# The cast of twelve weights' high part on GpSimd instead of ScalarE, in an attention and mixer kernel

## The chip, the cores and the metric

The kernel runs on one core of one Trainium2 chip. The metric is the device time of one execution in microseconds. A core has five engines with an instruction queue each: TensorE (PE; its weight load is listed apart as PEld), VectorE (DVE), ScalarE (ACT), GpSimd (POOL) and SyncE (SP), which here issues the DMAs. GpSimd works on SBUF only, not on PSUM, in this kernel.

## The reference

Attention within chunks of 64 positions for 8 batches, 8 heads, 576 positions and head size 64, and then a mixer over the result:

```python
x    = attention(q, k, v)                      # per chunk of 64, [8, 576, 512], float32
xt   = x.transpose(0, 2, 1)
h    = np.maximum(xt @ w_tok1, 0.0) @ w_tok2   # over the 576 tokens, hidden size 256
u    = x + h.transpose(0, 2, 1)
h2   = np.maximum(u @ w_ch1, 0.0) @ w_ch2      # over the 512 channels, hidden size 1536
out  = u + h2
```

The four weights come as 64-bit floats. "First channel product" means `u @ w_ch1`, "second channel product" the one with `w_ch2`.

## The kernel before, in words

TensorE multiplies numbers of a reduced format, fp32r. To keep the precision of float32, each float32 operand is split into a high part (the operand cast to fp32r) and a low part (the operand minus the high part, again in fp32r). A product is then three matmuls into one PSUM tile: high by high, low by high, high by low (the list `THREE`).

The channel weights are cut into twelve slices each along the hidden size of 1536: `c1` slices for the first product and `c2` slices for the second, each 128 partitions by 512. They arrive as pairs of 32-bit words of a 64-bit float (`raw`), and are turned into float32 and split once, at the start of the program, in the order c1 0, c1 1, c2 0, c1 2, c2 1, ... Each slice passes these steps (line, engine, tile):

1. `words_scalar`: the upper words scaled into `wtop` (L189) and the lower words into `low` (L190), both on ScalarE
2. `words_clamp`: `wtop` clamped on VectorE (L196) and cast into the other half of `low` on ScalarE (L199)
3. `words_shift`: `wtop` shifted on VectorE (L203)
4. `words_add`: `low` added to `wtop` on VectorE (L209, a custom instruction); `wtop` then holds the float32 weight
5. `split_high`: the high part, `wtop` cast into `kept[:, 0]` on ScalarE (L251 for c1, L254 for c2 and for the token weights)
6. `split_low`: the low part, `wtop - kept[:, 0]` into `kept[:, 1]` on VectorE (L262)

`wtop` has four buffers, and one is free again after step 6. The generator `conversion` staggers the steps of successive slices: the clamp of slice i, shift and add and high part of slice i-1, low part of slice i-2. The token weights (`t1`, `t2`) pass steps 1 to 4 at the very start, and are split later, through the same functions.

Beside this, TensorE works on the first batch's 576 rows in two halves of 288: for each of the twelve slices, `ch1` computes the first product of both halves (L663, PSUM `ps_c`) and `ch2` the second of the first half (L705, PSUM `acc`). Between them, the result of the first product is rectified and split: its high part `gh` on ScalarE (L674), its low part `gl` on VectorE (L675); the second half's result is kept as `g` (L671) and split later (L685, L686). Attention of the second batch is spread over the same time: scores (L313), maximum, difference and exponential (L329, L332, L336), the transposed probabilities `pt` (L407), the product with v (L426), the division (L447), a transposition through memory (L379 and DMAs), and the split of the result, `xh` on ScalarE (L467) and `xl` on GpSimd (L468). After that come seven further stretches of rows, the later ones with sums of slices (`ring`), in which no weight of the input is converted any more; GpSimd helps there with additions and low parts (L653, L716, L988, L997, L1004, L1077, L1111, L1121).

What sets the order: the queues of TensorE, ScalarE and VectorE are written out by hand up to the first token products (about 45 us). Then a planner that simulates the program orders these queues, until TensorE's is written by hand again for the later rows. SyncE's queue is in program order throughout; GpSimd's is the planner's throughout.

Of the kernel before, what the change touches and what calls it, by code (L numbers as in the profile page):

```python
# [91 lines left out]
def attention_mixer_kernel(ctx, tc, qk_in, vo_in, v_in, w1_in, w2_in, wc1_in, wc2_in, out):  # L92
# [19 lines left out]
    nc = tc.nc  # L112
# [33 lines left out]
    weights, tops, lows = {}, {}, {}  # L146
# [78 lines left out]
    def conversion():  # L225

        for i in range(len(plan) + 2):
            if i < len(plan):
                prepare(i + 1 - len(prepared))
                words_clamp(i)  # L230
                yield
            if 0 < i <= len(plan):
                words_shift(i - 1)
                yield
            if 0 < i <= len(plan):
                words_add(i - 1)
                if i - 1 >= token:
                    split_high(i - 1)
                yield
            if token <= i - 2:  # L240
                split_low(i - 2)
                yield

    def split_high(i):

        key, _, _, n = plan[i]
        name = "kept_" + "_".join(map(str, key))
        kept = ctx.enter_context(tc.tile_pool(name=name, bufs=1, reuse_waits="tile"))
        if key[0] == "c1":
            parts = kept.tile([P, 2, 2, KH], F32R, name=name).rearrange("p j w n -> p w j n")  # L250
            nc.scalar.copy(out=parts[:, 0], in_=tops[i].rearrange("p (j n) -> p j n", j=2))  # L251
        else:
            parts = kept.tile([P, 2, n], F32R, name=name)
            nc.scalar.copy(out=parts[:, 0], in_=tops[i])  # L254
        tops[key, "parts"] = parts

    def split_low(i):
# [570 lines left out]
    def split(i):  # L828
        with ExitStack() as late:
            for engine in (nc.scalar.engine, nc.vector.engine):  # L830
                late.enter_context(tc.issue_after(last_of[engine]))
            split_high(i)
            split_low(i)
            if plan[i][0][0] == "t1" and ("t1", 4) in weights and not half_low:
                kept_half = const.tile([P, 2, DT], F32R, name="half_low")
                half_all.append(kept_half)
                for c in range(2):
                    nc.vector.tensor_scalar(
                        out=kept_half[:, c], in0=weights["t1", 4][:, 1].bitcast(F32),
                        scalar1=half_mask[:, c:c + 1], scalar2=None, op0=ALU.mult,  # L840
                    )
                    half_low.append(kept_half[:, c])
# [483 lines left out]
```

## Time and profile before

| | |
|---|---|
| median of 3 runs | 772.92 us (770.47, 772.92, 773.38) |
| the profiled execution | 771.12 us, span 769.3 us |
| busy: TensorE | 751.5 us |
| busy: VectorE, ScalarE, GpSimd | 440.4, 275.8, 193.8 us |
| the twelve `c2` casts | 34.4 to 99.2 us from the span's start |
| granted TensorE clock | 0.999 of full speed |

A row of a timeline gives start and duration in us, the engine, the line of the kernel, the operation, the tile written and those read, the shapes, the number of instructions, and in brackets the idle time of the engine before it with what ended it. A row of groups gives busy time in all, the mean of one in ns, and the idle time before them. A row of one line gives the shortest, median and longest duration in ns.

### The profile page before, as it was taken

The numbers are of one execution on the slowest core, as the hardware profiler recorded it, in microseconds if no ns is written. First come the engines' busy times: TensorE is split into PE (matmuls) and PEld (weight loads), VectorE is DVE, ScalarE is ACT, GpSimd is POOL, SyncE is SP. The second block draws the span as 40 slices with busy tenths as digits, with TensorE's granted clock in tenths as the row PEclk, the third lists the DMA queues.
The fourth block names the chain that finished last, engine by engine and source line by source line (L and its number), as shares of the span: only waits on it lengthen the run. The fifth ranks groups of instructions, "written<-read, shape, count | busy, mean of one in ns | idle before, by whom it ended". The sixth has DMA issues, their size and how long they took to land.

```text
span 769.3 us, 14611 instructions
## 1 busy us (share of the span) xinstructions
PE 751.5 (98%) x5742; PEld 631.9 (82%) x5742; DVE 440.4 (57%) x735; ACT 275.8 (36%) x505; POOL 193.8 (25%) x163
## 2 busy tenths in 40 slices
PE   7899999999999999999999999999999999999997
PEld 4589998878888887888888888988888888888886
DVE  5898946646537456596567653875344458333351
ACT  6899933332223334243242222432112133111310
POOL 0000002343446544021111162141212504212121
PEclk9999999999999999999999999999999999999999
DMA  9956245677945776828878872056344512534011
GB/s 356 407 211 216 76 152 194 214 244 245 294 151 183 219 238 194 260 73 262 277 250 271 270 251 72 2 188 209 126 156 145 172 49 86 188 124 148 4 52 51
DMA packets 93268, 139.94 MB, mean 182 GB/s; under 512 B 10832, under 2 KB 44880, under 8 KB 93200
## 3 DMA queue, kind: packets, MB, share of 16 engines
q1 hardware_dynamic: 93200, 139.02, 54.9%
q8 instruction: 45, 0.74, 0.4%
q14 instruction: 23, 0.19, 0.1%
HBM read 98.34 MB, written 39.71 MB: 179 GB/s over the span
## 4 chain that ended last, share of the span: by engine, by line
PE 84%; DVE 5%; ACT 5%; DMA 2%; issue 2%; SPq 1%; POOL 0%; POOLq 0%; ACTq 0%; DVEq 0%
PE acc L1098 25%; PE ps_p L1031 22%; PE acc L705 10%; PE ps_c L663 8%; PE ps_t L635 7%; PE ps_t L565 6%; PE ps_sv L356 2%; PE ps_sv L368 2%; DVE wtop L209 1%; PE sum L574 1%; ACT low L199 1%; ACT wtop L189 1%; ACT low L190 1%; DMA raw_t<-in_w 1%; DVE blocks L379 1%
## 5 line engine op out<-in xcount | busy, mean ns | idle before, releaser
L1098 PE MATMUL acc<-gh,kept_c 128*128 128x512 f32 (+1 forms) x576 | 176.2, 387 | 0.0
L1031 PE MATMUL ps_p<-bh,ring 128*128 128x512 f32 (+1 forms) x504 | 154.3, 387 | 0.0
L1098 PEld LDWEIGHTS acc<-gh,kept_c 128*128 128x128 f32 x576 | 107.4, 188 | 20.6
L1098 PE MATMUL acc<-gl,kept_c 128*128 128x512 f32 (+1 forms) x288 | 111.1, 386 | 0.0
L1031 PEld LDWEIGHTS ps_p<-bh,ring 128*128 128x128 f32 x504 | 94.0, 188 | 18.2
L1031 PE MATMUL ps_p<-bl,ring 128*128 128x512 f32 (+1 forms) x252 | 97.2, 386 | 0.0
L705 PE MATMUL acc<-gh,kept_c 128*128 128x288 f32 (+1 forms) x384 | 95.3, 347 | 1.0 <-ACT gh L674 1.0
L468 POOL TENSOR_TENSOR xl<-x,xh 128x512 fp32r<-128x512 f32 x28 | 38.6, 1392 | 165.7 <-ACT xh L467 154.5
L705 PEld LDWEIGHTS acc<-gh,kept_c 128*128 128x128 f32 x384 | 64.0, 188 | 9.9 <-ACT gh L674 1.4
L1121 POOL TENSOR_TENSOR sum<-snap,sum 128x512 f32<-128x512 f32 (+1 forms) x18 | 23.5, 1305 | 180.2 <-ACT snap L1116 165.6
L1098 PEld LDWEIGHTS acc<-gl,kept_c 128*128 128x128 f32 x288 | 54.0, 188 | 10.4
L705 PE MATMUL acc<-gl,kept_c 128*128 128x288 f32 (+1 forms) x192 | 60.4, 343 | 1.2 <-DVE gl L686 1.2
L663 PE MATMUL ps_c<-uh,kept_c 128*128 128x512 f32 x192 | 59.8, 393 | 0.0
L1031 PEld LDWEIGHTS ps_p<-bl,ring 128*128 128x128 f32 x252 | 47.3, 188 | 9.0
L336 ACT ACTIVATE pr<-pr 128x512 f32<-128x512 f32 x36 | 22.8, 632 | 81.3 <-DVE pr L332 77.3
L1126 ACT ACTIVATE gh<-c 128x512 fp32r<-128x512 f32 (+1 forms) x36 | 22.4, 623 | 81.8 <-DVE c L1121 78.2
L1116 ACT COPY snap<-ps_p 128x512 f32<-128x512 f32 (+1 forms) x36 | 20.8, 578 | 82.2 <-PE ps_p L1031 82.2
L675 DVE SCALAR_TENSOR_TENSOR gl<-ps_c,gh 128x512 fp32r<-128x512 f32 (+1 forms) x36 | 21.7, 604 | 46.2 <-ACT gh L674 46.1
L1127 DVE SCALAR_TENSOR_TENSOR gl<-g,gh 128x512 fp32r<-128x512 f32 (+1 forms) x36 | 33.2, 951 | 22.2 <-ACT gh L1126 16.4
L663 PE MATMUL ps_c<-both,kept_c 128*128 128x288 f32 x288 | 43.9, 298 | 0.1
L663 PEld LDWEIGHTS ps_c<-uh,kept_c 128*128 128x128 f32 x192 | 35.5, 188 | 7.5 <-DVE rl L583 0.2
L663 PEld LDWEIGHTS ps_c<-both,kept_c 128*128 128x128 f32 x288 | 39.6, 188 | 0.8 <-ACT g L671 0.3
(134 smaller groups left out, 1272.4 us busy)
## 6 DMA issues: line engine op xcount, KB each, us to landing
ring<-w SPq DMA_DIRECT2D x126, 256.0 KB, 4.1
qk<-in_qk SPq DMA_DIRECT2D x36, 512.0 KB, 5.3
far<-blocks SPq DMA_DIRECT2D x63, 256.0 KB, 3.0
raw_c<-in_wc SPq DMA_DIRECT2D x24, 512.0 KB, 9.6
pf<-far SPq DMA_DIRECT2D x124, 64.0 KB, 2.7
v<-in_v SPq DMA_DIRECT2D x27, 256.0 KB, 5.3
xt<-far SPq DMA_DIRECT2D x96, 64.0 KB, 2.1
w<-sparts SPq DMA_DIRECT2D x24, 256.0 KB, 2.8
```

The source lines that it names most:

```text
L336: nc.scalar.activation(out=pr, in_=pr, func=AF.Exp, scale=1.0 / float(D) ** 0.5)
L468: nc.gpsimd.tensor_tensor(out=xl, in0=t["own"], in1=xh.bitcast(F32), op=ALU.subtract)
L565: nc.tensor.matmul(ps, lhsT=lhsT, rhs=rhs, start=(n == 0 and q == 0), stop=(n == len(mt) - 1 and q == len(terms) - 1),)
L635: nc.tensor.matmul(ps[:, at:at + n], lhsT=lhsT[:, cols], rhs=rhs, start=(q == 0), stop=(q == len(terms) - 1),)
L663: nc.tensor.matmul(ps[:, :width], lhsT=weights["c1", f][:, wi, k // 2, k % 2 * P:(k % 2 + 1) * P], rhs=u[ui][k], start=(k == 0 and q == 0) ...
L675: nc.vector.scalar_tensor_tensor(out=gl, in0=ps[:, :width], scalar=0.0, in1=gh.bitcast(F32), op0=ALU.max, op1=ALU.subtract)
L705: nc.tensor.matmul(accs[e], lhsT=weights["c2", f][:, wi, e * P:(e + 1) * P], rhs=g[gi], start=(f == 0 and q == 0), stop=(f == NFC - 1 and ...
L1031: nc.tensor.matmul(ps, lhsT=w[:, wi, j * P:(j + 1) * P].bitcast(F32R), rhs=u[ui][j], start=j == 0 and q == 0, stop=j == 1 and q == 2,)
L1098: nc.tensor.matmul(accs[e], lhsT=weights["c2", f][:, wi, e * P:(e + 1) * P], rhs=g[gi], start=start and q == 0, stop=stop and q == 2,)
L1121: (engine or nc.vector).tensor_tensor(out=c, in0=a, in1=b, op=ALU.add)
L1126: nc.scalar.activation(out=gh, in_=c, func=AF.Relu)
L1127: nc.vector.scalar_tensor_tensor(out=gl, in0=c, scalar=0.0, in1=gh.bitcast(F32), op0=ALU.max, op1=ALU.subtract)
```

## The change

In `split_high`, the high part of the `c2` slices is written by GpSimd's `tensor_copy` instead of ScalarE's `copy`. The `c1` slices and the token weights keep ScalarE.

```diff
         else:
             parts = kept.tile([P, 2, n], F32R, name=name)
-            nc.scalar.copy(out=parts[:, 0], in_=tops[i])
+            if key[0] == "c2":
+                nc.gpsimd.tensor_copy(out=parts[:, 0], in_=tops[i])
+            else:
+                nc.scalar.copy(out=parts[:, 0], in_=tops[i])
         tops[key, "parts"] = parts
```

## The prediction

> **What bounds the kernel now.** I read the busy shares first, then the chain, then a table of stretches around the changed casts, then what the matmul queue waited for.
>
> ```profile
> span 769.3 us, 14611 instructions
> PE 751.5 (98%) x5742; PEld 631.9 (82%) x5742; DVE 440.4 (57%) x735; ACT 275.8 (36%) x505; POOL 193.8 (25%) x163
> PE 84%; DVE 5%; ACT 5%; DMA 2%; issue 2%; SPq 1%; POOL 0%; POOLq 0%; ACTq 0%; DVEq 0%
> ```
>
> TensorE is busy for 751.5 of 769.3 us, so all its gaps together are 17.8 us, and no help to another engine can give more. The 10% of the chain that runs over VectorE and ScalarE lies in the first part. The next answer cuts the span into stretches: length, then busy time (and instructions) of PE, weight load, DVE, ACT, POOL, then granted clock, DMA share and GB/s.
>
> ```profile
> 34.00:100.00 66.00, 64.52 (x570) 58.52 (x569) 59.59 (x122) 62.24 (x118) 2.99 (x2) 1.00 0.52 182
> 100.00:125.00 25.00, 23.50 (x222) 22.11 (x222) 13.15 (x28) 9.32 (x23) 5.11 (x5) 1.00 0.51 152
> 125.00:245.00 120.00, 119.17 (x1074) 100.08 (x1073) 64.78 (x108) 37.07 (x72) 46.24 (x40) 1.00 0.67 224
> 350.00:769.30 419.30, 413.85 (x2549) 348.01 (x2547) 214.72 (x321) 104.62 (x188) 99.82 (x74) 1.00 0.47 152
> ```
>
> The change works in 34 to 100 us. There ScalarE (62.24 of 66) and VectorE (59.59 of 66) are both nearly full, GpSimd is empty (2.99), and yet TensorE is busy for 64.52. Its waits, longest first (total us, times, longest), in 34 to 125 us:
>
> ```profile
> PE acc L705 <- DVE gl L686: 1.2, 1, 1.2
> PE acc L705 <- ACT gh L674: 1.0, 3, 0.4
> PE ps_v L426 <- ACT pt L407: 0.6, 2, 0.4
> ```
>
> So 2.8 us of TensorE's time in this stretch were spent waiting for the engines that the change touches, 1.6 us of it directly for ScalarE. That is the ceiling of the gain there.
>
> **The change part by part.**
>
> *Removed from ScalarE: twelve casts.*
>
> ```profile
> L254 ACT CAST kept_c<-wtop x12: 617/625/705, 34.4 to 99.2; 128x512 fp32r<-128x512 f32 x12
> 80.33 0.66 ACT L254 CAST kept_c<-wtop 128x512 fp32r<-128x512 f32 x1
> 80.84 0.84 ACT L190 ACTIVATE low<-raw_c 128x512 int16<-128x512 uint32 x1
> ACT kept_c L254 <- DVE wtop L209: 2.1, 4, 0.7
> ```
>
> One lasts 0.625 us, but the next instruction starts 0.51 us after it (80.33 to 80.84), so ScalarE gets 12 x 0.51 = 6.1 us back, and also the 2.1 us in which it stood at these casts for VectorE's add. Its 62.24 us become some 56 of 66. On TensorE's path this is worth at most the 1.6 us of waits for gh and pt; those waits also hang on VectorE (ScalarE's order holds casts and exponentials that wait for it), so I take a third, -0.5 us, between 0 and -1.6. The line's five other casts (the token weights) stay on ScalarE. No DMA is issued by the step, and none reads the twelve tiles: SyncE's queue is not touched.
>
> *Added on GpSimd: twelve casts of 128x512.* The trace has no GpSimd instruction with one input. The nearest rows on that engine have two inputs of the same size:
>
> ```profile
> L988 POOL TENSOR_TENSOR wsum<-kept_c x12: 1277/1294/1746, 154.7 to 283.4; 128x512 f32<-128x512 f32 x12
> 110.05 1.29 POOL L468 TENSOR_TENSOR xl<-x,xh 128x512 fp32r<-128x512 f32 x1 [14.82 <-ACT xh L467]
> 124.85 0.40 PE L565 MATMUL ps_t<-xl,kept_t 128*128 128x512 f32 x1
> ```
>
> I bound the cast by ScalarE's 0.62 us below and by 1.29 us above, and take 0.9 us, near the middle: the engine is the slower one, but has half as much to read. That is 12 x 0.9 = 10.8 us (7.4 to 15.5) on an engine with 63 us free in the stretch. Queued behind the casts stand GpSimd's subtractions for the token product; the third starts at 110.05, and TensorE first reads one at 124.85, so a delay of a cast or two is covered by 13 us.
>
> [...]
>
> *Added: a new wait.* The subtraction of line 262 on VectorE now waits for GpSimd. Behind it in VectorE's order stand the next weights' steps and the low halves gl that TensorE reads. What it has to spare is seen in these rows:
>
> ```profile
> 81.79 0.67 DVE L262 TENSOR_TENSOR kept_c<-wtop,kept_c 128x512 fp32r<-128x512 f32 x1
> 98.44 0.68 DVE L209 CUSTOM_DVE_ANT_0 wtop<-wtop,low 128x1024 uint16<-128x1024 uint16 x1
> 99.04 0.45 DVE L675 SCALAR_TENSOR_TENSOR gl<-ps_c,gh 128x288 fp32r<-128x288 f32 x1
> 100.03 0.64 DVE L262 TENSOR_TENSOR kept_c<-wtop,kept_c 128x512 fp32r<-128x512 f32 x1
> 100.87 0.56 PE L705 MATMUL acc<-gl,kept_c 128*128 128x288 f32 x3
> 108.88 1.74 PE L663 MATMUL ps_c<-both,kept_c 128*128 128x288 f32 x12
> ```
>
> The cast at 80.33 has its subtraction at 81.79, 1.46 us after its start; the last weight's add ends at 99.12 and its subtraction starts at 100.03, 0.91 us later. A cast of 0.9 us fits in both; one of 1.29 us would hold the last by some 0.4 us. The weights themselves are ready early: the last is complete at 100.67, while the last group but one of the first channel product starts at 108.88 and the second product's use comes after it. A conversion that ends 8 us late is therefore hidden. Cover that is thin is gl's: it is done at 99.49 and read at 100.87, 1.4 us.
>
> *Added: GpSimd in VectorE's way.* In the stretch GpSimd ran twice, and both times a VectorE instruction was long:
>
> ```profile
> 72.36 1.69 POOL L468 TENSOR_TENSOR xl<-x,xh 128x512 fp32r<-128x512 f32 x1 [70.83 <-ACT xh L467]
> 73.11 1.21 DVE L196 TENSOR_SCALAR wtop<-wtop 128x512 f32<-128x512 f32 x1 [0.23 <-ACT wtop L189]
> 93.93 1.30 POOL L468 TENSOR_TENSOR xl<-x,xh 128x512 fp32r<-128x512 f32 x1 [19.89 <-ACT xh L467]
> 94.06 1.72 DVE L209 CUSTOM_DVE_ANT_0 wtop<-wtop,low 128x1024 uint16<-128x1024 uint16 x1
> 95.87 0.62 ACT L254 CAST kept_c<-wtop 128x512 fp32r<-128x512 f32 x1 [0.52 <-DVE wtop L209]
> L196 DVE TENSOR_SCALAR wtop<-wtop x24: 373/418/1214, 24.7 to 93.4; 128x512 f32<-128x512 f32 x24
> L209 DVE CUSTOM_DVE_ANT_0 wtop<-wtop,low x24: 643/682/1718, 28.9 to 98.4; 128x1024 uint16<-128x1024 uint16 x24
> ```
>
> Against their medians the two lost 1.214 - 0.418 = 0.80 and 1.718 - 0.682 = 1.04 us, each until shortly after GpSimd's instruction ended (74.05 and 95.23); ScalarE then stood 0.52 us at 95.87. Together 1.83 us for two GpSimd instructions of 1.29 us undisturbed: 0.71 us lost per us held. Twelve casts of 0.9 us would cost VectorE 12 x 0.9 x 0.71 = 7.7 us (5.3 at 0.62 us, 11.0 at 1.29 us; if each held VectorE for all its length, 15.5; nothing, if it always found VectorE in another kind of work, but these four groups are most of the stretch):
>
> ```profile
> L209 DVE CUSTOM_DVE_ANT_0 wtop<-wtop,low 128x1024 uint16<-128x1024 uint16 x22 | 15.9, 726 | 0.2
> L262 DVE TENSOR_TENSOR kept_c<-wtop,kept_c 128x512 fp32r<-128x512 f32 x22 | 14.9, 678 | 0.2
> L196 DVE TENSOR_SCALAR wtop<-wtop 128x512 f32<-128x512 f32 x20 | 9.0, 455 | 4.0 <-ACT wtop L189 3.8
> L203 DVE TENSOR_SCALAR wtop<-wtop 128x512 int32<-128x512 int32 x21 | 8.6, 417 | 1.0 <-ACT low L199 1.0
> ```
>
> 15.9 + 14.9 + 9.0 + 8.6 = 48.4 of 59.59 us. VectorE has 66 - 59.59 = 6.4 us free, 4.8 of it waiting for ScalarE's own steps, which the change brings earlier. So 7.7 us overrun it by 1.3 us, about what gl's 1.4 us of cover takes. I charge +0.9 us on TensorE's path for places where cover is thinner (0 to 7.7 us, below).
>
> [...]
>
> *Sum.* -0.5 + 0.9 = +0.4 us. The profiled execution took 771.12 us (span 769.3 and 1.8 us around it); the runs shown are 770.47, 772.92 and 773.38, so it lies 1.8 us under their median. With the four executions' mean of 771.97 the sum gives 772.4 us, no measurable change.
>
> **The rivals.**
>
> *VectorE becomes the bound (slower).* Place: 52 to 100 us, gl and the attention steps behind blocked conversion steps. It decides when the loss passes 6.4 + 1.4 = 7.8 us, a cast of 7.8 / (12 x 0.71) = 0.92 us. At 1.29 us the excess is 11.0 - 7.8 = 3.2 us, TensorE has nothing after 100 us to win it back with, and the time is 775.2 us; at a full block 15.5 - 7.8 = 7.7 us, 779.7 us. For it speak the two stalled rows; against it that neither delayed a matmul much, and the weights' 8 us of cover.
>
> *TensorE's waits go (small gain).* A quick cast, hidden in VectorE's other work, and ScalarE early everywhere: all 2.8 us go, 769.2 us. Against it: 1.2 us of them wait for gl at line 686 behind five token-weight subtractions on VectorE, which no moved cast touches:
>
> ```profile
> 118.48 3.56 DVE L262 TENSOR_TENSOR kept_t<-wtt,kept_t 128x512 fp32r<-128x512 f32 x5
> 121.97 0.44 DVE L686 TENSOR_TENSOR gl<-g,gh 128x288 fp32r<-128x288 f32 x1
> ```
>
> *The planned order shifts.* Engine orders after the hand-written part come from a planner that sees other durations, and it may order later work otherwise. From 125 us TensorE is idle for 0.8 us to 245 and 5.5 us after 350, the end included, so a gain there is worth at most a few us; a loss has no such bound, but other engines have much free time. I give it 4 us either way: 768 or 776 us.
>
> *The change moves nothing,* since ScalarE's load never reached TensorE: 772.0 us, inside the forecast.
>
> **How the numbers follow.** Forecast (hidden, -1 to +1.5 us: 771 to 773.5) 0.52; VectorE the bound 0.28; waits gone 0.13; order shifted 0.07. 0.5% is 3.9 us, about what a measurement of this kernel can tell from no change. Slower: of VectorE's case some two thirds (longer than 1.29 us held, or more than 0.71 lost per us), 0.18, and half of the last, 0.04: 0.22. Faster: 0.06 from waits gone together with a better order, 0.04 from the last: 0.10. The rest, 0.68, is the same. The range runs from 768.5 (all waits gone) to 777.5 us (midway between VectorE's two prices), which leaves out about 2 in 10.
>
> **What would show it.** Right: line 254 with twelve GpSimd casts of 0.6 to 1.3 us in 30 to 100 us; ScalarE some 6 us lighter in 34 to 100; stretched L196, L209 and L262 on VectorE, 5 to 11 us in sum; TensorE still at 64 us of 66. Wrong: a cast well over 1.3 us; TensorE's waits for gl or gh in 52 to 125 us grown beyond 3 us; or the time moved after 125 us, where no step of mine works.

## The result, and the profile after

The changed kernel takes 777.28 us (median of seven executions, 773.26 to 778.41), the kernel before 771.38 us in the same session (769.77 to 773.38): a ratio over all executions of 1.006, with a 95% interval of 1.0043 to 1.0078 (the two medians alone would give 1.0076). It is slower by more than the 0.5% named in the prediction, where no change was forecast. The profiled execution after took 777.69 us with a span of 775.9 us, 6.6 us more than the profiled one before. Line numbers above 254 are larger by 3 in the changed kernel; the new cast is line 255.

First the page of the changed kernel: span, busy times and chain.

```profile
span 775.9 us, 14639 instructions
PE 754.7 (97%) x5742; PEld 633.3 (82%) x5742; DVE 438.1 (56%) x735; ACT 270.9 (35%) x493; POOL 202.5 (26%) x175
PE 90%; DMA 4%; DVE 2%; SPq 1%; ACT 1%; issue 1%; POOLq 0%; POOL 0%; ACTq 0%; DVEq 0%
```

TensorE's idle time rose from 17.8 to 775.9 - 754.7 = 21.2 us, and its busy time by 3.2 us for the same 5742 matmuls: half of the loss is waiting, half is matmuls that lasted longer in sum. The chain holds more of TensorE and less of VectorE and ScalarE than before, so neither of these became the bound. The same stretches as in the prediction (length, busy time of PE, weight load, DVE, ACT, POOL, then clock, DMA share, GB/s):

```profile
34.00:100.00 66.00, 66.00 (x518) 59.79 (x517) 57.42 (x116) 55.23 (x104) 11.72 (x13) 1.00 0.46 164
100.00:125.00 25.00, 25.00 (x295) 24.08 (x294) 15.40 (x29) 9.31 (x21) 5.92 (x6) 1.00 0.45 144
125.00:245.00 120.00, 113.05 (x1025) 92.98 (x1024) 60.16 (x106) 37.07 (x71) 39.91 (x36) 0.99 0.71 230
```

Up to 125 us the changed kernel does all that the change could hope for: TensorE has no gap left (64.52 + 23.50 became 66.00 + 25.00, the whole 3.0 us that stood open), and ScalarE is 7.0 us lighter. The new order has a share in this: with the change alone, in the old order (experiment 1), TensorE still stands idle for 2.0 us there. The loss comes after that: 113.05 busy of 120 us where it was 119.17, while the changed casts end at 95 us. TensorE's waits over the whole span, longest first, and the place of the new long one:

```profile
PE ps_v L429 <- ACT pt L414: 4.2, 5, 1.4
PE acc L708 <- ACT gh L677: 3.9, 1, 3.9
PE ps_s L316 <- DMA qk<-in_qk: 2.7, 2, 2.4
PE ps_t L638 <- DVE u L644: 1.7, 1, 1.7
```

```profile
173.99 0.47 SPq L488 DMA_DIRECT2D xc<-x  x1
178.94 1.26 ACT L497 CAST xr<-xc 64x512 fp32r<-64x512 f32 x2 [9.24 <-DMA xc<-x]
180.10 0.59 ACT L677 ACTIVATE gh<-ps_c 128x512 fp32r<-128x512 f32 x1
180.74 0.94 PE L708 MATMUL acc<-gh,kept_c 128*128 128x512 f32 x2 [3.86 <-ACT gh L677]
```

Read upwards: the matmul waits 3.86 us for gh; gh stands on ScalarE behind two casts into xr; these waited 9.24 us for the transfer of xc, which SyncE issued at 173.99 us. In the trace before, that transfer was issued 8.7 us earlier. ScalarE stood 6.70 us at such a cast there, too, but no matmul waited for gh behind it:

```profile
165.27 1.36 SPq L485 DMA_DIRECT2D xc<-x  x2
168.60 0.62 ACT L494 CAST xr<-xc 64x512 fp32r<-64x512 f32 x1 [6.70 <-DMA xc<-x]
```

What xc holds is not late: the division that writes it starts at nearly the same time. What is late is SyncE's queue, which issues in program order, and in which transfers of attention results (pf among them) stand ahead of xc. First the division, then pf, each before and after:

```profile
159.53 0.68 DVE L447 TENSOR_TENSOR x<-ps_sv,zs 128x512 f32<-128x512 f32 x1
160.13 0.68 DVE L450 TENSOR_TENSOR x<-ps_sv,zs 128x512 f32<-128x512 f32 x1
155.51 1.75 SPq L390 DMA_DIRECT2D pf<-far  x4
164.74 1.75 SPq L393 DMA_DIRECT2D pf<-far  x4
```

SyncE runs 7 to 15 us late from the second batch's first result on (issued at 71.04 us before, at 83.35 us after) until xc. The second batch's attention is late in the changed kernel: its first division (x, VectorE) and the three after it start at other times, before and after:

```profile
L447 DVE TENSOR_TENSOR x<-ps_v,zi x4: 681/688/694, 68.8 to 129.5; 128x512 f32<-128x512 f32 x4
L450 DVE TENSOR_TENSOR x<-ps_v,zi x4: 684/692/692, 80.4 to 136.0; 128x512 f32<-128x512 f32 x4
```

It is late because of TensorE's order. Counted in the traces, the four products with v of these tiles stand behind 96, 240, 378 and 484 channel matmuls (both products) in TensorE's queue before, and behind 132, 348, 456 and 534 after. SyncE's queue holds the same transfers in the same order in both. The last view is the granted clock in stretches of 2 us behind the wait:

```profile
180.00:182.00 2.00, 1.26 (x3) 0.65 (x4) 1.97 (x4) 0.69 (x2) 0.00 (x0) 0.78 0.84 252
182.00:184.00 2.00, 2.00 (x6) 1.52 (x6) 1.75 (x4) 0.63 (x1) 0.00 (x0) 0.50 0.91 233
184.00:186.00 2.00, 2.00 (x38) 1.45 (x36) 1.71 (x4) 0.96 (x3) 0.17 (x1) 0.87 0.83 320
```

At 0.78, 0.50 and 0.87 TensorE loses 2 x (0.22 + 0.50 + 0.13) = 1.7 us more; the trace before has no such stretch between 100 us and its last matmul. The two new waits (3.9 us for gh, 1.7 us for u) and the clock's 1.7 us are 7.3 us; against them stand the 3.0 us won before 125 us. Of the net loss of 6.6 us some 2.3 us are left, in waits and matmuls that I did not trace one by one.

### The profile page after: what moved, and what is told of

Read it like the earlier page. It is cut to its first block, busy times and chain, and to the rows that moved or that the text cites. A ratio compares the mean times of both kernels' runs of the same rounds, so it can differ in the third digit from the quotient of the medians.

```text
span 775.9 us, 14639 instructions
## 1 busy us (share of the span) xinstructions
PE 754.7 (97%) x5742; PEld 633.3 (82%) x5742; DVE 438.1 (56%) x735; ACT 270.9 (35%) x493; POOL 202.5 (26%) x175
## 4 chain that ended last, share of the span: by engine, by line
PE 90%; DMA 4%; DVE 2%; SPq 1%; ACT 1%; issue 1%; POOLq 0%; POOL 0%; ACTq 0%; DVEq 0%
PE acc L1101 25%; PE ps_p L1034 22%; PE ps_c L666 13%; PE acc L708 11%; PE ps_t L638 6%; PE ps_t L568 5%; DMA far<-blocks 2%; PE ps_sv L359 2%; PE ps_sv L371 2%; PE ps_t L611 1%; SPq L393 1%; PE sum L577 1%; PE ps_v L429 1%; DMA pf<-far 1%; DMA raw_t<-in_w 1%; PE ps_t L605 1%
```

## The experiments

Theories: O, the planner gave TensorE another order, and this costs the time; V, GpSimd's casts hold VectorE up; both named in the prediction, V with the greater chance. Each ratio is to the kernel before, on the same chip, from five rounds, with its 95% interval.

**1 and 2. Change and order taken apart.** The queues of TensorE, VectorE, ScalarE and GpSimd are held in a listed order by edges that only order the issue; the text of the kernel is otherwise the changed one (1) or the one before (2).

```diff
         attention_mixer_kernel(tc, *args)
+        hold_order(nc, tc)
```

> The changed casts, with every queue (TensorE, VectorE, ScalarE, GpSimd) held in the order that the kernel before had; only the twelve casts are new in GpSimd's queue. Theory O (the planner, seeing ScalarE free, drew a new order in which the second batch's attention comes behind channel matmuls, and that order costs the 4 to 6 us): the time is that of before, ratio 1.000 (0.997 to 1.003), and TensorE's 3.9 us wait near 175 us is gone. Theory V (GpSimd's casts stand in VectorE's way, or VectorE waits for them): the loss stays, ratio 1.005 to 1.008, with TensorE's waits for gl or gh in 52 to 125 us at 4 us or more. In both, VectorE's steps at lines 196, 209 and 262 are stretched by 3 to 8 us in sum.

> The casts back on ScalarE, with every queue held in the order that the changed kernel had; only the twelve casts are put back into ScalarE's queue. Theory O: slow without any cast on GpSimd, ratio 1.004 to 1.010 (776 us, or a little more as ScalarE carries its 6 us again), with the wait of 3 to 5 us near 175 us. Theory V: the time of before, ratio 0.998 to 1.002.

The casts on GpSimd in the old order: 0.9998 (0.9988 to 1.0008). The casts on ScalarE in the new order: 1.0126 (1.0113 to 1.0139). So the loss belongs to the order, and V is out: with the casts on GpSimd and everything in its old place, nothing is lost. Two expected sizes need the profile of the first, in its stretches and GpSimd's rows beside VectorE's:

```profile
34.00:100.00 66.00, 65.32 (x571) 58.98 (x572) 62.08 (x123) 56.93 (x107) 13.07 (x14) 1.00 0.51 183
67.90 0.73 POOL L255 CAST kept_c<-wtop 128x512 fp32r<-128x512 f32 x1 [5.96 <-ACT low L190]
68.06 1.10 DVE L209 CUSTOM_DVE_ANT_0 wtop<-wtop,low 128x1024 uint16<-128x1024 uint16 x1
83.98 0.68 POOL L255 CAST kept_c<-wtop 128x512 fp32r<-128x512 f32 x1 [2.92 <-DVE wtop L209]
84.11 1.10 DVE L265 TENSOR_TENSOR kept_c<-wtop,kept_c 128x512 fp32r<-128x512 f32 x1
56.96 1.56 POOL L255 CAST kept_c<-wtop 128x512 fp32r<-128x512 f32 x1 [7.76 <-DVE wtop L209]
```

The stretching is real (1.10 us against 0.68, each until about half a microsecond after the cast ended), but VectorE's load grew by only 62.08 - 59.59 = 2.5 us for twelve casts, which its 6.4 free us took up. It goes the other way, too: the cast at 56.96 us took 1.56 us beside three VectorE instructions that kept their usual 0.68, 0.68 and 0.45 us. In all, the twelve casts took 9.9 us, where twelve of the shortest, 0.61 us, would take 7.3; these 2.6 us fell on GpSimd, which had them to spare. The second kernel is slower than the changed one, and slower than the 1.004 to 1.010 that I had expected: in the new order the casts on GpSimd gain about 0.66% (1.0126 against 1.006), in the old order nothing that can be measured. Its wait at the same place:

```profile
PE acc L705 <- ACT gh L674: 4.8, 3, 3.4
```

**3. Which queue's order.** The changed kernel with TensorE's queue alone held in the order before; the other queues are the planner's.

> All twelve casts on GpSimd, TensorE's queue alone held in the order of the kernel before; the planner orders VectorE, ScalarE and GpSimd around it. If TensorE's order is what counts in theory O: ratio 0.998 to 1.002. If ScalarE's or VectorE's order is (gh and gl placed late among conversion steps): 1.004 to 1.007, with TensorE's waits for gh or gl above 5 us.

0.9998 (0.9985 to 1.001). TensorE's old order is enough to undo the loss; the orders that the planner then drew for the other three queues cost nothing that can be measured.

**4. The wait that was found.** The changed kernel in its own order, with the two casts into xr and the subtractions behind them moved behind the next gh and gl.

> The changed kernel with every queue held in its own order, except that the two casts of xr at line 497 (which wait for a copy by DMA) and the two subtractions that read them on VectorE stand behind the next high and low part (gh, gl) instead of ahead of them. Theory O with the place seen in the trace (ScalarE's queue stands at those casts for a DMA that SyncE issued 9 us later than before): TensorE's 3.9 us wait and the slow clock behind it go, ratio 1.000 to 1.002. Rival (the wait moves on: the attention is late anyway and TensorE stands at the next step that needs it): ratio 1.004 to 1.006.

A miss: 1.0085 (1.0071 to 1.0099), above both expected ranges. The wait moved on, as the rival had it, to the next attention steps in TensorE's queue, and the clock fell there:

```profile
PE ps_sv L359 <- issue: 3.7, 1, 3.7
PE ps_sv L371 <- ACT pt L410: 3.4, 3, 2.4
186.00:188.00 2.00, 1.25 (x33) 1.13 (x34) 0.74 (x2) 0.70 (x2) 1.05 (x1) 0.50 0.89 349
```

So ScalarE's queue was only the place where the lateness first showed; a step moved there does not make the attention or SyncE's transfers earlier.

**5 and 6. Attention given priority.** The planner is left free, but ranks the attention steps ahead.

```diff
-            {"ready": ready, "part": part, "split": split}[job](*of)
+            with tc.high_priority() if job == "part" else ExitStack():
+                {"ready": ready, "part": part, "split": split}[job](*of)
```

> The changed casts with the planner free again, but the steps of the second batch's attention traced with a higher priority, so that the planner puts them ahead of channel matmuls when both are ready. Theory O: the loss goes, ratio 0.998 to 1.002. Theory V: 1.005 to 1.008, as the casts are where they were.

> The same kernel as the one with the attention steps given priority, to see what its usual execution near 776.9 us holds that the profiled one of 773.6 us did not. Theory C: a wait of TensorE of 3 us or more between 100 and 200 us with 3 us and more at a granted clock of 0.50 behind it, ratio 1.005 to 1.0075. Rival: waits as in the profiled one (2.1 us at most) and a granted clock a little under 1 spread over the span.

A miss: 1.0062 (1.0049 to 1.0075), and 1.0051 (1.0032 to 1.0071) when run again, although the products with v now stand behind 84, 240, 384 and 479 channel matmuls, nearly as before the change. This is in the range that I had written for V, which experiment 1 rules out; so the attention's place alone does not bring the old time back. The first profile was of the quickest execution (773.6 us) and showed little; the second, of the slowest (779.0 us), shows where time can go. The same instruction, in the first and then the second:

```profile
108.59 0.70 PE L429 MATMUL ps_v<-v,pt 64*64 64x65 f32 x32 [1.04 <-ACT pt L410]
122.65 0.80 PE L708 MATMUL acc<-gl,kept_c 128*128 128x288 f32 x4 [2.06 <-DVE gl L689]
```

```profile
110.30 1.15 PE L429 MATMUL ps_v<-v,pt 64*64 64x65 f32 x32 [2.94 <-ACT pt L410]
112.00:114.00 2.00, 2.00 (x10) 2.00 (x10) 1.36 (x2) 0.62 (x1) 0.57 (x1) 0.50 0.90 346
126.88 1.33 PE L708 MATMUL acc<-gl,kept_c 128*128 128x288 f32 x4 [2.08 <-DVE gl L689]
128.00:130.00 2.00, 2.00 (x10) 2.00 (x10) 0.54 (x2) 0.58 (x2) 0.00 (x0) 0.50 0.84 240
```

A wait of 1.04 us was 2.94 us in the slower execution, where SyncE waited 2 us longer for a transfer ahead of it; the clock fell to 0.50 there, and once more after a wait of 2.08 us that had cost no clock in the quicker one (2.06 us). This order removes the 3.9 us wait and has two others, behind which the clock fell in one execution and not in the other. How often it falls, no run shows.

**7 and 8. Fewer casts.** Only slices 0 and 1 on GpSimd, and only slices 2 to 11, with the planner free:

```diff
-            if key[0] == "c2":
+            if key[0] == "c2" and key[1] < 2:
```

> Only the first two of the twelve casts on GpSimd (slices 0 and 1, at about 34 and 41 us), the planner free. In TensorE's queue this puts the second batch's attention late, as the whole change does: 536 matmuls of the two channel products stand ahead of the first joint scores-and-values step, where the kernel before has 504 and the changed kernel 560. Theory O (what counts is the order drawn, not the casts): slower although ten casts of twelve stay, ratio 1.002 to 1.008. Theory V (each cast on GpSimd costs): a sixth of the loss, ratio 0.999 to 1.002.

> Only slices 2 to 11 cast on GpSimd, the planner free. In TensorE's queue the attention stays early (500 channel matmuls ahead of the first joint step, where the kernel before has 504). Theory O: the time of before, ratio 0.997 to 1.002, although ten of the twelve casts are moved. Theory V: five sixths of the loss, ratio 1.004 to 1.007.

Two casts cost 1.0122 (1.0109 to 1.0135), ten 1.0038 (1.0024 to 1.0052), twelve 1.006. Both miss the ranges of both theories: two casts cost more than either allowed, and ten casts, at 1.0038, lie between them, although the attention stands early in that order. A cost per cast cannot give this; a new draw of the order each time can. Each has one long wait at another place, with the clock at 0.50 behind it. First the kernel with two casts, then the one with ten:

```profile
PE ps_t L638 <- DVE u L644: 5.3, 1, 5.3
154.00:156.00 2.00, 1.16 (x3) 0.97 (x4) 1.45 (x4) 1.34 (x3) 0.43 (x1) 0.50 0.61 180
```

```profile
PE ps_t L638 <- DVE rl L586: 3.3, 1, 3.3
150.00:152.00 2.00, 2.00 (x6) 1.52 (x6) 0.69 (x1) 0.55 (x2) 1.28 (x1) 0.50 1.05 301
145.85 0.71 DVE L382 STREAM_TRANSPOSE blocks<-pr 128x512 f32<-128x512 f32 x1 [5.45 <-DMA far<-blocks]
147.41 0.68 DVE L586 SCALAR_TENSOR_TENSOR rl<-ps_t,rh 128x512 fp32r<-128x512 f32 x1
```

With ten casts, rl (the low half that TensorE waits for) stands on VectorE behind a transposition that waited 5.45 us for a transfer.

**9. One place put right.** The kernel with ten casts, held in its own order, with that rl ahead of the transposition. (The expectation calls rl a reciprocal; it is the low half of a split.)

> The kernel with slices 2 to 11 on GpSimd, held in its own order on every queue, but on VectorE the reciprocal of the second block's sums (rl, done at 147.4 us there) stands ahead of the transposition that waited 5.45 us for the transfer of far. Theory (this one place in VectorE's order makes the 3.3 us wait of TensorE and the 0.50 clock behind it): both go, and the time falls from 1.0038 to 0.997 to 1.001 of the kernel before. Rival (the wait moves to the next attention step, as it did with the xr casts moved later): 1.003 to 1.005.

1.0023 (1.0007 to 1.0039), between the two expected ranges, so by the times it tells nothing apart. The profile, of the quickest of its twelve executions (span 769.6 us against 774.1), is clear on the place: the 3.3 us wait is gone, no wait over 1.1 us stands between 30 us and the end, and no stretch from 100 to 340 us has a clock under 0.98.

**10. Work in place of the wait.** The changed kernel, held in its own order, with one group of 12 first-product matmuls issued twice, just ahead of the waiting matmul.

```diff
-        for k in range(NDT):
+        for k in [k for _ in range(times) for k in range(NDT)]:
```

> The changed kernel with its own order of instructions on every queue, but one group of 12 matmuls of the first channel product (about 2.9 us) is issued a second time on TensorE, just ahead of the matmul that waited 3.9 us for gh in the changed kernel; its result is written over by the same values. So TensorE does 2.9 us of work more, in place of most of the wait. Theory C (the wait costs itself and then again, in the slower clock of 0.50 that followed each wait of 3.3 us and more in the kernels so far): the wait falls to about 1 us, no stretch at 0.50 follows, and the time is shorter than the changed kernel's by 1.5 to 3 us, a ratio of 1.001 to 1.004. Rival F (the low clock has another cause and stays): the wait is filled, the stretch at 0.50 stays, ratio 1.005 to 1.007. Rival W (the wait moves on by 2.9 us because ScalarE's chain is held up behind the added work): ratio 1.009 to 1.011.

The profiled span is 773.6 us, 2.3 us shorter than the changed kernel's with 2.9 us more work in it, together 5.2 us; the wait shrank by 3.86 - 0.25 - 0.17 = 3.4 us and the clock's 1.7 us are back:

```profile
178.40 0.73 PE L708 MATMUL acc<-gh,kept_c 128*128 128x512 f32 x2 [0.25 <-ACT gh L677]
179.31 0.50 PE L708 MATMUL acc<-gl,kept_c 128*128 128x512 f32 x1 [0.17 <-DVE gl L678]
182.00:184.00 2.00, 0.51 (x32) 0.37 (x27) 1.43 (x5) 1.30 (x4) 0.51 (x1) 1.00 0.73 281
```

So far theory C, and rival F's low clock is not there. The ratio over all executions does not bear C out: 1.0054 (1.0035 to 1.0072) lies in the range of F and above that of C, and the interval holds the changed kernel's 1.006. The profile, which is of the median execution (775.37 us), shows the clock at 1.00 behind the filled wait in that execution; that it pays over many executions is not shown.

**11 and 12. A better order.** The prediction saw a 1.2 us wait for gl behind token-weight subtractions. Here the two subtractions for `t2` are moved behind the next four gl and the masks on VectorE, in the old order, with the casts on GpSimd (11) and on ScalarE (12).

> All twelve casts on GpSimd, all queues held in the order of the kernel before, but on VectorE the two subtractions of the second token weight (1.5 us) stand behind the next four low parts and the two masks instead of ahead of them. TensorE's 1.2 us wait at 122 us for a low part goes: ratio 0.997 to 0.999 against before, 1 us under the same kernel without this. If that wait was already covered by something later, ratio 1.000.

> The casts on ScalarE as before and before's order on every queue, with the two subtractions into t2 moved behind the next four gl and masks on VectorE, as in the kernel that had this with the casts on GpSimd (0.999). If that kernel's 0.9 us came of the subtractions alone: 0.998 to 0.9995 here too. If the casts on GpSimd were needed for it (ScalarE free at that place): 0.9995 to 1.001.

0.999 (0.9979 to 1.0002) and 0.9979 (0.9965 to 0.9993). The wait for gl is gone in both. The second is quicker than both given kernels by a little, without the change: what gain there is comes of the two moved instructions. The first cannot be told from no change.

## Why the prediction was wrong

*The step that failed* is "the planned order shifts", a rival with a chance of 0.07. The sum of the forecast, and both of its terms, took the order before as fixed; experiments 1 and 3 show that with this order the forecast of no change holds (0.9998), and 1 and 2 that the order is the loss. The rival had the sign open and a size of 4 us; the 776 us it gave for a worse order is 1.3 us under what came. What it leaned on, that the other engines have much free time after 125 us, does not bound a wait: an engine that is 30% busy still stands behind one late transfer in its own queue (ScalarE, 37.07 us busy of 120, stood 9.24 us for xc). The sign I had named for a wrong reading, time that moves after 125 us, is what came. That the median, 777.28 us, still lies under the 777.5 us at which the range ends is luck: that end came from VectorE's prices, and VectorE is not where the time went. The lower end, 768.5 us, is called all waits gone, which the rivals price at 769.2 us.

*ScalarE's casts removed, -0.5 us.* Right for the load and the waits. ScalarE fell from 62.24 to 56.93 us in the old order (the prediction: some 56), and TensorE's waits for gh and pt in 34 to 125 us from 1.6 to 0.5 us, rows of the first experiment:

```profile
PE acc L708 <- DVE gl L689: 1.2, 1, 1.2
PE acc L708 <- ACT gh L677: 0.3, 1, 0.3
PE ps_v L429 <- ACT pt L410: 0.2, 1, 0.2
```

That is -1.1 us of waits, within the bounds 0 to -1.6. The time shows no such gain: 0.9998 with its interval is -0.9 to +0.6 us, which leaves room for the -0.5 us and does not show it. The 1.2 us for gl stayed, as the rival of the vanishing waits had it.

*The cast on GpSimd, 0.9 us.* Too long; the median is 0.72 us in the changed kernel, nearer to the lower bound. One of the twelve, at 67.42 us, took 1.90 us, beyond the upper bound; the two VectorE steps that ran wholly within it (67.82 and 68.42 us) kept 0.68 and 0.42 us, much as beside the one of 1.56 us above. No matmul waited for it:

```profile
L255 POOL CAST kept_c<-wtop x12: 611/718/1896, 34.6 to 94.7; 128x512 fp32r<-128x512 f32 x12
```

The shortest took 0.61 us, about ScalarE's shortest of 0.62 us, which was the lower bound.

*GpSimd in VectorE's way, 7.7 us and +0.9 us on the path.* The term that was mis-sized most: 2.5 us, under its lower end of 5.3, and nothing on the path. The loss per microsecond held is near what I took where the two meet (0.42 us for a cast of 0.7, 0.6 instead of 0.71), but it was charged to all twelve casts. Some ran beside instructions that kept their usual time (0.68, 0.68 and 0.45 us beside the cast at 56.96 us), some took longer themselves (the 2.6 us of experiment 1). With 2.5 under the 7.8 us from which the rival "VectorE becomes the bound" decides, that rival, with 0.28, is out. The rows show an instruction of one engine lasting longer beside one of the other: VectorE's 1.10 us instead of 0.68 at 68.06 and 84.11 us, GpSimd's 1.56 us at 56.96 us, where the shortest cast took 0.61. That VectorE would lose time to each of the twelve casts was my step, and it failed.

*The new wait, the weights' spare time.* Right: no wait of TensorE for a weight shows, and from 34 to 125 us there is none at all. In the changed kernel the conversion even ended earlier, at 96 instead of 101 us, while the attention came later.

## What to carry to other kernels

Where a planner orders the queues, a small move has two effects, its own and that of a new order, and here both together were +0.4% to +1.2% in four kernels that the planner ordered anew, while the move's own could not be measured in the old order (0.9998, 0.9988 to 1.0008); hold the order and run it once before believing either. Resource sums tell whether an engine is overrun, not who will be late: for a kernel whose TensorE is 98% busy, look for the long chain through memory (here attention, SyncE's transfers in program order, cast). To put this chain back to its place was not enough here (1.0062 and 1.0051); to hold TensorE's whole order was (0.9998). And a wait of TensorE of 3 us should, by these runs, be priced at its length and about 1.7 us or more of lost clock behind it (1.7 us behind the waits of 3.3, 3.4 and 3.9 us, 3.4 us behind the one of 2.9 us).

## What the runs showed of the hardware

I had not expected the granted clock to fall at a single wait of TensorE in a busy stretch. In the stretches of 2 us from 100 to 282 us of the fourteen profiles, it fell to 0.50 during or just behind waits of 2.9, 3.3, 3.4, 3.7 (with one of 2.4 close behind it), 3.9 and 5.3 us. It also fell at the end of one of 2.08 us, but not behind the same wait of 2.06 us in another execution, nor behind any of 2.0 us and less. Worked out from the stretches of 2 us (what is missing from full speed, over 0.5), it stayed there for 3.4 us each time, or for twice that: 2 x 0.85 / 0.5 = 3.4 us in the changed kernel, 2 x (0.10 + 3 x 0.50 + 0.11) / 0.5 = 6.8 us with two casts on GpSimd. From what length of a wait on the clock falls, these runs do not show: it fell at 2.08 us in one execution and not at 2.06 us in another.

The mean clock of an execution does not tell whether such a fall happened. The clock was also low early on: in the first profile of experiment 5 it was at 0.50 from 10 to 14 us and at 0.60 from 14 to 16 us. The changed casts in the old order had a mean of 0.992 at 770.13 us, with 1.00 from 34 to 100 us and in every stretch of 2 us from 100 to 282 us; the changed kernel, with its fall in 180 to 186 us, had a mean of 0.997 at 777.69 us.
